# Nyström attention with an MLP behind it: batch 1's first scores and turned block in other places, and batch 2's last spread later

## The chip, the cores and the metric

The kernel runs on one core of a Trainium2 chip. The time is device microseconds of one execution; five executions of the kernel before gave 312.87 to 313.04, with a median of 312.96. The profile is of one such execution. Its engines are TensorE (PE, with its weight loads as PEld), VectorE (DVE), ScalarE (ACT), GpSimd (POOL) and SyncE (SP), which issues most of the transfers.

## The reference

Inputs are q, k and v (8 batches, 8 heads, 576 positions, 64 wide), a layernorm gain g and the weights w_ch1 (512x2048) and w_ch2 (2048x512), all in float32. The output is 8x576x512.

```python
q_lm = q.reshape(B, H, 32, 18, D).mean(axis=3)     # k_lm alike: 32 landmarks
A, Bm, C = sm(q, k_lm), sm(q_lm, k_lm), sm(q_lm, k)  # softmax of scale * a b^T
Z = Bm^T / (norm1(Bm) * norminf(Bm) + 1e-6)
for _ in range(6):
    Z = 2 * Z - Z @ Bm @ Z
x = A @ Z @ C @ v                                   # heads put side by side: 512 wide
xn = (x - mean) / sqrt(var + 1e-6) * g
out = x + relu(xn @ w_ch1) @ w_ch2
```

So each batch has an attention part of many small matrices, with a chain of six dependent steps in its middle, and then 576 rows of a large MLP.

## The kernel before

The order in which each engine gets its instructions is the order in which the program writes them; nothing rearranges them afterwards. Since TensorE works through one list, the art of this kernel is what stands beside what: while one batch's attention waits for VectorE or ScalarE, TensorE is given matmuls of the MLP for rows that are finished already.

**The MLP stream.** The 4608 rows are 36 blocks of 128, in nine groups of four. `mlp()` is a generator. Each of its steps is one matmul: `psh` is the first layer (x is brought to f16 as `xn`, turned as `xnT`, multiplied with `w`, which is w_ch1 scaled by g, and `relu` leaves `hT`), and `pso` the second (from `hT` and w_ch2). `ot` adds x to the result on VectorE, and SP stores it. In the first group the first-layer matmuls take 256 columns, in the later ones 512. The turning of xn is done by TensorE in the first two groups (`psxt`); later a DMA transpose queued on SP does it (L843). From the fifth group on, the second layer is computed in a form with fewer products (`second_layer`, with `pspa`, `pspe` and `pspc`). `fill(n)` takes n steps from the stream.

**The attention.** Batch 0 is computed alone at the start (`attention(0)`, a generator that yields between its stages), batch 1 with the first steps of the stream beside it, and then come the sets (2), (3, 4), (5, 6) and (7) through `attention2`. Two heads of a batch lie side by side on 128 partitions, and four heads make one half, w = 0 or 1.

For batches 0 and 1, `turn_tile(b, w, nm)` turns one half of q or k: nine transposes on TensorE into `pst`, copied by ScalarE into `xT`. For batch 1 it does so in two parts of five and four, with two tiles of the pool `psM`, which has three buffers and serves `psh`, `psxt`, `pso` and the warm matmuls too. `sums(b, w, i, n16)` adds up the landmarks of one half, nine matmuls of 64 columns into `pss`. `scores_of_q(w)` computes eight matmuls into `psa` (in `ps2`, two buffers) and an exponential `ea` on ScalarE. `warm(n, cols)` issues n matmuls on zeros, whose result nobody reads. The iteration step is eight matmuls `psn` on TensorE, then `st` on VectorE, which the next step needs. Behind each of the six steps of batch 0 one more piece is issued, listed in `extra` (L399 and L400), and then what the first sequence of the program (L1117 to L1160) puts there, such as `turn_tile(1, 0, "q")`. Behind the steps come `pszc`, `zcbd` and the rows: `psy` (the product of `zcbd` and `ea`), divided into `xblk`, then `negm`, `xn` and `psxt`.

At the same time SP loads w_ch1 in eight pieces (`wstg`) and GpSimd scales them by g into `w` in pieces of 512 columns; the first `psh` takes them as they come.

**The sets.** For sets 2 and later `Coming` holds the loads, the casts to f16 on GpSimd (`nat`) and the jobs: `xT` by VectorE's own 32x32 transposes, sums `part` by VectorE (`part<-xT`, or `asum` and `s` on GpSimd, turned as `sT`), and the spread: `psl`, two matmuls that put the landmarks in place. `prepare(c, casts, jobs)` takes so many casts and jobs of a set, and issues the next loads on SP as staging buffers come free (tiles `stg` of q, k and v; later sets load into `ring`). `steps` is a table with one row a set and one entry (fills, casts, jobs) for each yield of `attention2`: so many stream steps, then so many casts and jobs of the next set. Ahead of batch 2's attention stand a loop that interleaves its last jobs with six fills each, and the loop at L1208 with two fills of 6 and 15 steps, behind each of which a cast of the set (3, 4) is issued. The last spread of batch 2 comes behind them.

So a number of fills in this table decides both where TensorE's attention matmuls stand among the stream's, and when SP's loads, GpSimd's casts and VectorE's jobs of the next set are issued among the stream's own `xn`, `ot` and stores.

Of the kernel before, what the change touches and what calls it, by code (L numbers as in the profile page):

```python
# [20 lines left out]
def kernel(  # L21
# [52 lines left out]
    def MM(o, l, r, rb=0, cb=0, start=True, stop=True, skip=False):  # L74
        keep(nc.tensor.matmul(o, l, r, start=start, stop=stop, tile_position=(rb, cb),  # L75
                              skip_group_check=(skip or cb != 0)))

    def TR(o, i_, idn):
        keep(nc.tensor.matmul(o, i_, idn, is_transpose=True, tile_position=(0, 0)))  # L79


    def load(src, b, u, queue, t=None):
        t = t or stage.tile([P, 2, NJ, D], FP32, name="stg", tag="stg")
        keep(queue.dma_start(
            out=t[:],
            in_=src[b, 4 * u:4 * u + 4].rearrange("(r e) (t j) d -> (e t) r j d", e=2, j=NJ)))
        return t
# [8 lines left out]
    def load_v(b):  # L96
        for u in range(U):
            raw[b]["v", u] = load(v, b, u, nc.sync)
# [124 lines left out]
    def fetch_w1():  # L223
        coming = []
        for i in range(10):
            if i < 8:
                f, half = divmod(i, 2)
                coming.append(w_stage(w1_src[:, 2 * half:2 * half + 2, ts(f, DM)]))
            if i >= 2:
                f, half = divmod(i - 2, 2)  # L230
                stg = coming.pop(0)
                for c in range(2):
                    k = 2 * half + c
                    pool.tensor_scalar(out=w1_16[:, k, ts(f, DM)], in0=stg[:, c, :],
                                       scalar1=g_sb[:, k:k + 1], scalar2=0.0,
                                       op0=ALU.mult, op1=ALU.add)
# [25 lines left out]
    def warm(n, cols):  # L262
        idle = psM.tile([P, 512], FP32, name="idle", tag="pm")
        for _ in range(n):
            MM(idle[:, 0:cols], zeros[:, 0:P], zeros[:, 0:cols])
# [11 lines left out]
    def sums(b, w, i, n16):  # L277
        for j in range(NJ):
            MM(nat_pss[b, i][:, w, :], n16[:, j, :, :].rearrange("p r d -> p (r d)"),
               pm16[:], start=(j == 0), stop=(j == NJ - 1), skip=True)  # L280

    def turn_part(w, nm, part):
        j0, j1 = ((0, 5), (5, NJ))[part]
        n16 = nat_tiles[1, nm, w]
        if part == 0:
            early_xT[1, nm, w] = aprep.tile([P, NJ, P], FP16, name="xT", tag="xT" + nm,
                                            bufs=5 if nm == "q" else 4)
        pst = psM.tile([P, 5, P], FP16, name="pst", tag="pm")
        for j in range(j0, j1):
            TR(pst[:, j - j0, :], n16[:, j, :, :].rearrange("p r d -> p (r d)"), ident16[:])  # L290
        scalar.copy(early_xT[1, nm, w][:, j0:j1, :], pst[:, 0:j1 - j0, :])

    def turn_tile(b, w, nm):
        i = 0 if nm == "q" else 1
        if b == 1:
            if not i and w == 0:
                pss = ps1.tile([P, 2, U, 64], FP32, name="pss", tag="p1")
                nat_pss[b, 0], nat_pss[b, 1] = pss[:, 0, :, :], pss[:, 1, :, :]
            turn_part(w, nm, 0)
            turn_part(w, nm, 1)  # L300
            return None
        if w == 0:
            nat_pss[b, i] = psM.tile([P, U, 64], FP32, name="pss" + nm, tag="pm")
        n16 = nat_tiles[b, nm, w]
        t = aprep.tile([P, NJ, P], FP16, name="xT", tag="xT" + nm, bufs=5 if nm == "q" else 4)
        early_xT[b, nm, w] = t
        last = (w, i) == (U - 1, 1)
        pst = ps2.tile([P, NJ, P], FP16, name="pst", tag="p2")
        if last:
            sums(b, w, i, n16)  # L310
        for j in range(NJ):
            TR(pst[:, j, :], n16[:, j, :, :].rearrange("p r d -> p (r d)"), ident16[:])
        if not last:
            scalar.copy(t[:], pst[:])
            sums(b, w, i, n16)
        return t, pst

    def attention(b):
# [6 lines left out]
        def p2(shape, dtype, name):  # L325
            return ps2.tile(shape, dtype, name=name, tag="p2")
# [48 lines left out]
        def product(w):  # L375
            if not pscv_:
                pscv_.append(p2([P, W, D + 1], FP32, "pscv"))
            natv = natv_of[b]
            for j in range(NJ):
                for h in range(4):  # L380
                    r, e = divmod(h, 2)
                    rows = ds(64 * e, 64)
                    MM(pscv_[0][ds(32 * h, 32), w, :], ect[w][rows, j, ds(32 * r, 32)],
                       natv[rows, w, j, r, :], rb=64 * e, cb=32 * h,
                       start=(j == 0), stop=(j == NJ - 1), skip=True)

        def scores_of_q(w):
            psa = p2([P, NJ, 64], FP32, "psa")
            for (j0, j1) in ((0, 8), (8, NJ)):
                for h in range(4):  # L390
                    r, e = divmod(h, 2)
                    rows = ds(64 * r, 64)
                    MM(psa[ds(32 * h, 32), j0:j1, :], klm[rows, w, ds(32 * e, 32)],
                       early_xT[b, "q", w][rows, j0:j1, ds(64 * e, 64)], rb=64 * r, cb=32 * h)
            t = aexp.tile([P, NJ * 64], FP16, name="ea", tag="e")
            act(t[:], psa[:].rearrange("p j t -> p (j t)"), AF.Exp, scale=sc_A)
            ea.append(t)

        extra = [None, lambda: product(0), lambda: product(1), lambda: scores_of_q(0),  # L399
                 lambda: scores_of_q(1), None]  # L400
        if first:
            warm(2, 384)
            yield "gram"
# [706 lines left out]
    def fill(n):  # L1110
        for _ in range(n):
            if not next(stream, False):
                return

    def scaled_by_pe():
        psg = psM.tile([P, KCH], FP32, name="psg", tag="pm")
        TR(psg[:], g_rows[:], ident4[:])  # L1117
        dve.tensor_copy(out=g_sb[:], in_=psg[:])

    warm(36, 160)  # L1120
    a0 = attention(0)
    for w, nm in [(w, nm) for w in range(U) for nm in ("q", "k")]:
        last_tile = turn_tile(0, w, nm)
# [6 lines left out]
    for it in range(6):  # L1130
        next(a0)
        if it == 0:
            warm(1, 384)
        elif it == 1:
            scaled_by_pe()
            fetch_w1()
        elif it == 5:
            turn_tile(1, 0, "q")
    next(a0)
    turn_tile(1, 0, "k")  # L1140
    next(a0)
    next(a0)
    sums(1, 0, 0, nat_tiles[1, "q", 0])
    sums(1, 0, 1, nat_tiles[1, "k", 0])
    turn_tile(1, 1, "q")
    sums(1, 1, 0, nat_tiles[1, "q", 1])
    warm(1, 256)
    load_v(1)
    fill(1)
    warm(1, 256)  # L1150
    fill(1)
    turn_tile(1, 1, "k")
    next(a0)
    fill(2)
# [3 lines left out]
    fill(4)  # L1158
    next(a0)
    a1 = attention(1)  # L1160
    next(a1)
    next(a1)
# [9 lines left out]
    def prepare(c, casts, jobs):  # L1172
        for _ in range(casts):
            if c.casts and (c.parts[c.casts[0]][0] == "v" or len(c.n16) < 8):
                c.next_cast()
                while sum(len(x.stg) for x in sets) < (4 if len(sets[1].casts) > 8 else 3):
                    left = [x for x in sets if x.loads]
                    if not left:
                        break
                    left[0].next_load()  # L1180
        for _ in range(jobs):
            c.next_job()
# [23 lines left out]
    while len(sets[0].jobs) > 1:  # L1206
        prepare(sets[0], 1, 1)
        fill(6)  # L1208
    for count in (6, 15):
        fill(count)  # L1210
        prepare(sets[1], 1, 0)

    steps = [[(10, 1, 0), (12, 1, 1)] + 6 * [(6, 1, 1)] + [(8, 1, 1)] + 5 * [(6, 0, 0)]]
    steps += [[(6, 1, 0), (10, 1, 0), (12, 1, 0), (12, 1, 0), (5, 1, 0), (5, 1, 0)] + 4 * [(4, 1, 0)] + [(8, 0, 0), (4, 0, 0), (4, 0, 0), (10, 0, 0)] + 7 * [(8, 1, 1)]]
    steps += [[(12, 1, 0), (14, 1, 1), (16, 1, 1), (16, 1, 1)] + 6 * [(5, 1, 1)] + [(6, 1, 1), (6, 1, 1), (12, 1, 1), (40, 1, 1)] + 7 * [(10, 1, 1)]]
    steps += [[(15, 0, 0), (18, 0, 0)] + 6 * [(8, 0, 0)] + [(10, 0, 0)] + 5 * [(9, 0, 0)]]
    mixing = mixes_of_w2()
# [58 lines left out]
```

## Time and profile before

| what | value |
| --- | --- |
| time of the kernel, median of five | 312.96 us (312.87 to 313.04) |
| time of the profiled execution | 312.96 us |
| its span, first to last instruction | 311.2 us |
| mean granted TensorE clock | 0.998 |
| TensorE busy | 301.7 us, 3475 matmuls |
| VectorE busy | 194.8 us |
| ScalarE busy | 155.7 us |
| GpSimd busy | 141.2 us |
| DMA moved | 50.36 MB, a mean of 162 GB/s |

The page lists busy times by engine, forty slices of the span, the DMA queues, the chain of work that ended last, and groups of instructions. In the lines of a timeline the first two numbers are the start and the time taken, in us; then come engine, line, operation, out<-in, shape and count, and in brackets the idle time ahead of it with what ended it. A run of instructions of one kind without a gap is one line. Times of single matmuls overlap, since they are pipelined: what a matmul costs TensorE in a run is the time from one start to the next, 216 ns for 128x512, 109 for 128x256, 55 for a 128x128 transpose. "issue" is a wait for which the profile shows no releaser.

### The profile page before, as it was taken

To read this page: it belongs to the slowest core of one execution; us is meant where nothing else is said; L and a number is where in the kernel's file an instruction comes from. 1 tells how busy PE (TensorE), PEld (TensorE's weight loads), DVE (VectorE), ACT (ScalarE), POOL (GpSimd) and SP (SyncE) were. 2 spreads that over 40 slices of the span, in tenths; PEclk is the share of its full clock that TensorE was granted. 3 is DMA by queue.
4 is the path that set the end of the run, shared out by engine and by line. 5 is a ranking of instruction groups with operands and counts; after the bars stand their busy time and mean duration, and the time that the engine had idled before them with its cause. 6 is when DMAs were issued, how large, how long until landed. Compare 5 with 4: busy or idle time off the path is not lost.

```text
span 311.2 us, 8486 instructions
## 1 busy us (share of the span) xinstructions
PE 301.7 (97%) x3475; PEld 178.9 (57%) x3475; DVE 194.8 (63%) x525; ACT 155.7 (50%) x309; POOL 141.2 (45%) x191
## 2 busy tenths in 40 slices
PE   7889999999999999999999999999999999999994
PEld 7557764553444534544454468547844874685583
DVE  3667228878785426899257697749635970671364
ACT  2566774469515871177354661693147506405600
POOL 4389878886988493598098412030003240000000
PEclk9999999999999999999999999999999999999999
DMA  7999999999995986750169401530050316105013
GB/s 273 392 386 385 386 388 253 328 343 308 297 194 105 299 239 185 101 205 0 37 96 246 98 1 35 135 68 5 2 135 13 57 43 141 21 3 135 0 36 101
DMA packets 38863, 50.36 MB, mean 162 GB/s; under 512 B 17572, under 2 KB 18088, under 8 KB 38824
## 3 DMA queue, kind: packets, MB, share of 16 engines
q1 hardware_dynamic: 38504, 49.43, 56.5%
q8 instruction: 27, 0.44, 0.6%
q10 hardware_dynamic: 320, 0.39, 0.4%
q14 instruction: 12, 0.10, 0.1%
HBM read 36.70 MB, written 9.44 MB: 148 GB/s over the span
## 4 chain that ended last, share of the span: by engine, by line
PE 92%; DMA 2%; DVE 2%; ACT 1%; issue 0%; SPq 0%
PE psh L75 42%; PE pso L75 18%; PE pspa L75 8%; PE pspe L75 6%; PE pspc L75 6%; PE psy L75 3%; DMA stg<-in_k_dram 2%; PE psn L75 2%; PE pscv L75 2%; PE psec L75 1%; PE psea L75 1%; PE psse L75 1%; DVE xblk L69 1%; PE psxt L79 1%; PE psa L75 0%; PE psl L75 0%
## 5 line engine op out<-in xcount | busy, mean ns | idle before, releaser
L75 PE MATMUL psh<-xnT,w 128*128 128x512 f16 (+1 forms) x640 | 136.7, 358 | 0.5 <-issue 0.2
L69 ACT ACTIVATE hT<-psh 128x512 f16<-128x512 f32 x144 | 84.7, 598 | 71.8 <-PE psh L75 71.2
L75 PEld LDWEIGHTS <-w 128*128 128x128 f16 x640 | 58.9, 98 | 56.2 <-issue 4.9
L75 PEld LDWEIGHTS <-hT 128*128 128x128 f16 x656 | 62.8, 98 | 30.3 <-issue 1.1
L75 PE MATMUL pso<-w,hT 128*128 128x512 f16 x256 | 61.1, 379 | 0.0
L69 POOL TENSOR_SCALAR xn<-xblk,negm,rstd 128x512 f16<-128x512 f32 x20 | 16.9, 855 | 66.9 <-DVE negm L69 33.1
L69 ACT ACTIVATE junk<-xblk,negm 128x512 f16<-128x512 f32 x36 | 25.9, 719 | 18.0 <-POOL negm L69 10.7
L69 DVE SCALAR_TENSOR_TENSOR xblk<-psy,rcpd 128x512 f32<-128x512 f32 (+1 forms) x40 | 27.6, 691 | 1.8
L69 DVE SCALAR_TENSOR_TENSOR st<-st,psn 128x128 f16<-128x128 f16 (+2 forms) x36 | 11.4, 317 | 22.6 <-PE psn L75 22.2
L69 DVE TENSOR_TENSOR hmix<-hT 128x256 f16<-128x256 f16 (+2 forms) x20 | 8.9, 444 | 21.6 <-ACT hT L69 21.6
L69 POOL CAST nat<-stg 128x1152 f16<-128x1152 f32 x15 | 17.1, 1147 | 6.2 <-DMA stg<-in_q_dram 4.1
L69 DVE STREAM_TRANSPOSE xT<-nat 128x576 uint32<-128x576 uint32 x24 | 18.4, 768 | 0.0
L69 DVE TENSOR_REDUCE part<-xT 128x32 f16<-128x576 f16 x26 | 18.3, 745 | 0.1
L69 DVE RECIPROCAL rcpd<-psy 128x8 f32<-128x8 f32 (+1 forms) x40 | 8.1, 202 | 15.6 <-PE psy L75 15.3
L69 DVE SCALAR_TENSOR_TENSOR ot<-pso,rstd,xblk 128x512 f32<-128x512 f32 x16 | 12.0, 747 | 7.8 <-PE pso L75 4.4
L75 PEld LDWEIGHTS <-hmix 128*128 128x128 f16 x160 | 15.6, 98 | 2.0 <-issue 0.2
L69 DVE TENSOR_TENSOR xblk<-pspa,xblk 128x256 f32<-128x256 f32 x38 | 14.0, 417 | 4.2 <-PE pspa L75 4.2
L69 POOL CAST nat<-ring 128x1152 f16<-128x1152 f32 x12 | 13.6, 1145 | 6.7 <-DMA ring<-in_k_dram 4.1
L75 PE MATMUL psy<-zcbd,ea 128*128 128x260 f16 (+1 forms) x80 | 15.4, 277 | 0.0
L69 POOL CAST natv<-stg 128x1152 f16<-128x1152 f32 x10 | 11.5, 1164 | 7.8 <-DMA stg<-in_v_dram 7.4
L75 PEld LDWEIGHTS <-st 32*32 32x32 f16 x448 | 5.6, 90 | 14.5 <-issue 7.6
L69 POOL TENSOR_TENSOR asum<-asum 128x256 f32<-128x256 f32 (+1 forms) x22 | 13.1, 595 | 1.7
(129 smaller groups left out, 383.0 us busy)
## 6 DMA issues: line engine op xcount, KB each, us to landing
wstg<-in_moe_w_ch_dram SPq DMA_DIRECT2D x16, 512.0 KB, 7.0
stg<-in_q_dram SPq DMA_DIRECT2D x10, 576.0 KB, 7.9
stg<-in_k_dram SPq DMA_DIRECT2D x10, 576.0 KB, 7.4
out_dram<-xblk SPq DMA_DIRECT2D x34, 128.0 KB, 2.3
out_dram<-ot SPq DMA_DIRECT2D x32, 128.0 KB, 3.3
stg<-in_v_dram SPq DMA_DIRECT2D x7, 576.0 KB, 9.3
ring<-in_k_dram SPq DMA_DIRECT2D x6, 576.0 KB, 5.1
ring<-in_q_dram SPq DMA_DIRECT2D x6, 576.0 KB, 5.8
```

Of the source, the lines that this page charges most:

```text
L69: return lambda *args, **kw: keep(getattr(self.engine, op)(*args, **kw))
L75: keep(nc.tensor.matmul(o, l, r, start=start, stop=stop, tile_position=(rb, cb), skip_group_check=(skip or cb != 0)))
L79: keep(nc.tensor.matmul(o, i_, idn, is_transpose=True, tile_position=(0, 0)))
```

## The change

Four edits, all of the order of issue; no operation is changed but the size and number of the warm matmuls.

1. `extra` of batch 0: the scores of q's second half go from behind the fifth iteration step to behind the sixth, and in the first sequence the turn of batch 1's first half of q from behind the sixth to behind the fifth.
2. Behind the first two row blocks of batch 0, the turn of q's second half comes first, then three warm matmuls of 512 columns (in all; before there were two of 256, each ahead of a stream step), the load of v and one stream step; the sums of the first halves of q and k stand behind it, then the second stream step, then the sum of q's second half. The sums of k's second half stay.
3. The second fill of the loop at L1208 is 20 steps instead of 15, so a cast of the set (3, 4) and the last spread of batch 2, and all attention behind it, stand five stream steps later.
4. In the second row of `steps` the last seven entries have 7 fills instead of 8, so each of the seven takes one stream step less.

```diff
         extra = [None, lambda: product(0), lambda: product(1), lambda: scores_of_q(0),
-                 lambda: scores_of_q(1), None]
+                 None, lambda: scores_of_q(1)]
...
-        elif it == 5:
+        elif it == 4:
             turn_tile(1, 0, "q")
     next(a0)
     turn_tile(1, 0, "k")
     next(a0)
     next(a0)
+    turn_tile(1, 1, "q")
+    warm(3, 512)
+    load_v(1)
+    fill(1)
     sums(1, 0, 0, nat_tiles[1, "q", 0])
     sums(1, 0, 1, nat_tiles[1, "k", 0])
-    turn_tile(1, 1, "q")
+    fill(1)
     sums(1, 1, 0, nat_tiles[1, "q", 1])
-    warm(1, 256)
-    load_v(1)
-    fill(1)
-    warm(1, 256)
-    fill(1)
     turn_tile(1, 1, "k")
...
-    for count in (6, 15):
+    for count in (6, 20):
         fill(count)
         prepare(sets[1], 1, 0)
...
-    steps += [[(6, 1, 0), (10, 1, 0), (12, 1, 0), (12, 1, 0), (5, 1, 0), (5, 1, 0)] + 4 * [(4, 1, 0)] + [(8, 0, 0), (4, 0, 0), (4, 0, 0), (10, 0, 0)] + 7 * [(8, 1, 1)]]
+    steps += [[(6, 1, 0), (10, 1, 0), (12, 1, 0), (12, 1, 0), (5, 1, 0), (5, 1, 0)] + 4 * [(4, 1, 0)] + [(8, 0, 0), (4, 0, 0), (4, 0, 0), (10, 0, 0)] + 7 * [(7, 1, 1)]]
```

## The prediction

> **What bounds the kernel now.** I read the busy shares and the clock row first, then the chain that ended last, then TensorE's waits, then its timeline wherever it pauses, and the other engines only there.
>
> ```profile
> span 311.2 us, 8486 instructions
> ...
> PE 301.7 (97%) x3475; PEld 178.9 (57%) x3475; DVE 194.8 (63%) x525; ACT 155.7 (50%) x309; POOL 141.2 (45%) x191
> ...
> PEclk9999999999999999999999999999999999999999
> ...
> PE 92%; DMA 2%; DVE 2%; ACT 1%; issue 0%; SPq 0%
> ```
>
> TensorE is busy for 301.7 of 311.2 us and carries 92% of the chain, so it is the bound. It idles 9.5 us: about 1.6 at the start (its first wait) and about 4.2 behind its last matmul, neither touched here, and some 3.7 in small pauses. A change of order can win only from those pauses, or add to them. The change touches the pauses at these places:
>
> ```profile
> 17.79 0.42 PE L75 MATMUL psa<-xT,klm 64*32 64x512 f16 x8 [0.48 <-ACT ea L69]
> ...
> 19.55 0.87 PE L79 MATMUL pst<-ident,nat 128*128 128x128 f16 x9 [0.41 <-ACT xT L69]
> ...
> 21.64 0.41 PE L75 MATMUL pss<-pm,nat 128*128 128x64 f16 x8 [0.48 <-issue]
> ...
> 23.88 0.40 PE L79 MATMUL psxt<-ident,xn 128*128 128x128 f16 x4 [0.40 <-DVE xn L69]
> ...
> 107.58 3.07 PE L75 MATMUL psh<-xnT,w 128*128 128x512 f16 x12
> ...
> 115.06 0.59 PE L75 MATMUL psh<-xnT,w 128*128 128x512 f16 x2 [0.22 <-issue]
> ...
> 160.89 3.41 PE L75 MATMUL pso<-w,hT 128*128 128x512 f16 x15
> 164.41 0.38 PE L75 MATMUL psh<-xnT,w 128*128 128x512 f16 x1
> ```
>
> Two kinds are seen. Some wait for another engine (ea, xT, xn). Others wait for nothing the profile names: at 21.64; inside the twelve psh from 107.58, which at the pace of 0.216 us from start to start would take 2.6 us and took 3.07; and before 115.06. Counted in the trace's list for TensorE, the instructions after these three pauses are numbers 706, 3009 and 3265: multiples of 256 apart, within one. I take them for late instruction blocks, and the DMA queues support it:
>
> ```profile
> q8 instruction: 27, 0.44, 0.6%
> ```
>
> The columns are packets, MB and share. 3475 matmuls and 3475 weight loads over 27 packets make 257 a packet. The packets before the three pauses start at 19.27, 106.95 and 112.51, which is 2.38, 2.46 and 2.55 us before TensorE goes on. So a packet becomes instructions about 2.5 us after its transfer.
>
> **Part 1, scores and first turn swapped (edit 1), sums behind the turned block, longer warm matmuls (edit 2).** The swap puts the nine transposes of batch 1's first block where psa waited 0.48 us for ea, and the second scores where pst waited 0.41 for xT. Rows 1 and 2 (psy, 20.26) move to about 19.6, and the chain psy, xblk, negm, xn, psxt, all behind it, by as much. Against that, the warm work grows from two matmuls of 0.109 (pace of 128x256 in psh rows) to three of 0.216: 0.65 for 0.22, so 0.43 more of work that computes nothing. It stands where TensorE waited for xn (0.40), so most of it replaces waiting. The 27 sums (about 29 ns each) and the transposes (55 each) change place only. Counted through, psxt(0) moves from 22.98 to about 22.2, psxt(1) from 23.88 to 23.25, and psh at 24.83 to about 24.4: the stage wants to gain 0.4 to 0.7.
>
> It cannot keep all of it. The first hidden layer is fed by GpSimd's scaling of w_ch1, and that by the DMA:
>
> ```profile
> 20.84 5.54 POOL L69 TENSOR_SCALAR w<-wstg,g_sb 128x512 f16<-128x512 f32 x8 [0.31 <-DMA wstg<-in_moe_w_ch_dram]
> 26.59 4.96 POOL L69 TENSOR_SCALAR w<-wstg,g_sb 128x512 f16<-128x512 f32 x7 [0.21 <-DMA wstg<-in_moe_w_ch_dram]
> ...
> 29.48 0.82 PE L75 MATMUL psh<-xnT,w 128*128 128x256 f16 x6
> ```
>
> The second run's first four operations feed the hidden columns that TensorE takes from 29.48 on. The last of them ends at 29.54 and its matmul starts at 29.81, with about 0.2 us of slack after the handover. SP issues the loads up to 58 us, those of v by `load_v(1)` among them, in the order of before. So I take −0.2; bounds −0.4 (if a smaller clash of VectorE's xn with GpSimd frees 0.2 more: one w operation takes 0.94 beside an xn, the median is 0.69) and +0.43 (the added warm work all on the path).
>
> The clock row is 9 in all forty slices (mean 0.998) with these pauses in it, so the longer warm work has no clock to win.
>
> **Part 2, the last spread of batch 2 five stream steps later (edit 3).** Five psh steps of 0.216, or 1.08 us, go ahead of psl(0) and everything attention does after it. The work only changes places: 0 by itself. The DMA and GpSimd side shift: on SP, a k load of batches 3 and 4, issued at 62.11, now stands behind two more output stores and the first turning of xn (before 64.50, 1.84 long), so it goes out between 64.5 and 66.3, about 3.4 us later in the middle. GpSimd's cast of that block comes later, with the cast and the xn of a block that stand behind it in order. GpSimd waits 2.08 us for a q load at 72.47 anyway, and xnT of the third group lands at 93.05 for a use at 95.0. With that cover I cost it 0; bounds −0.1 and +0.5.
>
> It also moves the second spread, of batches 3 and 4, by about 1.0:
>
> ```profile
> 95.68 0.49 DVE L69 TENSOR_TENSOR part<-sT 128x64 f16<-128x64 f16 x1
> 96.10 0.74 DVE L69 SCALAR_TENSOR_TENSOR ot<-pso,rstd,xblk 128x512 f32<-128x512 f32 x1
> ...
> 96.23 0.39 PE L75 MATMUL psl<-part,spread 128*128 128x256 f16 x2
> ```
>
> TensorE waits for VectorE here already, about 0.14. VectorE runs nearly without a gap from 87 to 97. Its rows start 1.0 later, and the ot of 0.74 that stood behind the last part now stands ahead of it; the rows' wait of 0.69 and the ot's of 0.26 shrink in return. I get part at about 97.4 for a psl wanted at 97.0: late by 0.4 instead of 0.14, taken as +0.3; bounds −0.14 and +0.7 (the whole ot).
>
> **Part 3, seven fills of 8 become 7 (edit 4).** The shift falls from five steps to −2 (5 − 7) over the rows of batches 3 and 4, and stays near there. Together with edits 1 and 2 it moves where the instruction blocks fall in the stream, and it moves the stores.
>
> The pauses near 109 and 115: one psh in each took 0.522 and 0.613 from start to start instead of 0.216, so 0.31 and 0.40 are lost. The packet for the first came only when a burst of ring loads had drained:
>
> ```profile
> 98.14 1.21 SPq L843 DMA_TRANSPOSE xnT<-xn  x1
> 99.45 1.85 SPq L84 DMA_DIRECT2D ring<-in_k_dram  x2
> 101.40 4.59 SPq L84 DMA_DIRECT2D ring<-in_q_dram  x2
> ```
>
> From 102.5 to 106.6 the DMA moves about 400 GB/s. With the change that block of 256 is entered about 1.2 us later and holds more of the quick attention matmuls, so only about 4.3 us instead of 5.8 lie between asking and needing. The stores ahead of the ring loads leave about 0.75 earlier, the burst drains by about 106.4, the block is there at about 108.9, wanted at 109.0. I take +0.15 where 0.31 stood. For 115.06 the block before it now lasts at least 6.2 us for a need of 5.65, so its 0.40 goes. Sum: −0.56; bounds −0.71 and +0.8 (the packet takes the full 5.8 again: 1.5 late, less the 0.71).
>
> The Trainium skill's page "Runtime: NRT & Kernel Launch", section "Instruction fetch mechanics", says that crossing a block of 256 instructions is "mostly hidden". By it this term would be 0 and the sum −0.17; the rows have three pauses of 0.65, 0.31 and 0.40 at such crossings, so the measurement decides.
>
> Last, 164.41: fifteen pso at pace would end at 164.13; psh of the fifth group waits about 0.27 for the last turning of its xn on the DMA queue. Two steps fewer before it put the second half of the products (pscv, 0.7 us) ahead of that psh, and the wait goes: −0.27; bounds −0.27 and +0.1.
>
> **Sum**, on the profiled execution's 312.96 (span 311.2 and 1.76 around it; it is also the median of the five runs): −0.2 + 0 + 0.3 − 0.56 − 0.27 = −0.73, so 312.2. I give back 0.1 for the two instructions the stream gains and for block crossings elsewhere that I have not followed: **312.3**.
>
> **The rivals.**
> (a) Slower, by the instruction packet at about 109. If the queue delays it for as long as before (5.8 us from asking), TensorE stands 1.5 us there. For it: the DMA is still at about 400 GB/s in that stretch. Against it: the loads come earlier. The sum becomes −0.2 + 0.3 + 0.8 − 0.27 = +0.6, or 313.6; with the early gain lost to the warm work (+0.43) 314.2. It decides from a packet after about 107.2 on.
> (b) No change: the early gain is all eaten (0 for −0.2), the second spread is late by the whole ot (+0.7), the pauses go (−0.56), xnT's wait goes (−0.27): −0.1, or 312.85. For it: VectorE's full stretch. Against it: two of its waits can shrink.
> (c) The late k load carries through GpSimd to xnT of the third group. It has 1.95 between landing and use; a delay of 3.4 that the 2.08 wait does not absorb would cost up to 1.5: about 313.7. Against it: the delayed cast is early in a chain with that wait behind it.
>
> **How the numbers follow.** What a measurement tells from no change is 0.2%, 0.63 us: faster is below 312.33, slower above 313.59. The forecast's case (early gain, pauses mostly gone) has 0.45, of which 0.40 lies below 312.33 and 0.05 above. (b) has 0.25, all within. (a) reaches from 313.6 to 314.2 and has 0.20, of which 0.15 lies above 313.59; (c) has 0.10, all above. That makes 0.40 faster, 0.35 same, 0.25 slower. The range goes from 311.8 (pauses all gone, the second spread no later than now) to 313.9, the middle of (a) and past (c); what is left out is half of (a) and a little below. The likeliest case alone: 311.8 to 312.7.
>
> **What would show it.** Right: psy near 19.6 and psh near 24.4, at 30 only about 0.2 ahead of before; psl of the second spread waiting about 0.4 for part; psh at a pace of 216 ns through 107 to 116; psh of group five directly behind pscv. Wrong: a pause above 0.5 us without a releaser between 98 and 116, waits of GpSimd's xn past 90 us, or new pauses where blocks of 256 now begin.

## The result, and the profile after

The changed kernel takes 313.91 us (median of 53 runs, most between 312.8 and 315.3) and the kernel before 312.88 (94 runs). The ratio is 1.0026, with a 95% interval of 1.0014 to 1.0037: about 0.8 us slower, where 0.6 faster was forecast. (This ratio, and those below, compare executions taken in the same sessions, so they are not the quotients of the medians given.) The profiled execution took 314.74, which is 0.8 above the median; it shows what can happen to this kernel, not its middle.

The page of the changed kernel:

```profile
span 313.0 us, 8490 instructions
...
PE 302.5 (97%) x3476; PEld 178.3 (57%) x3476; DVE 194.4 (62%) x525; ACT 155.8 (50%) x309; POOL 140.5 (45%) x191
...
PE 92%; DMA 2%; DVE 2%; issue 1%; SPq 0%; ACT 0%
```

TensorE is still the bound. "issue" in the chain has come up from 0% to 1%. The list of TensorE's waits from 33 us on names only that:

```profile
engine line waited for: us in total, times, longest us
PE psh L75 <- issue: 1.0, 1, 1.0
PE psea L75 <- issue: 0.7, 1, 0.7
```

TensorE's timeline at the places of the forecast:

```profile
19.50 0.82 PE L75 MATMUL psy<-zcbd,ea 128*128 128x260 f16 x4
...
21.89 0.60 PE L75 MATMUL idle<-zeros 128*128 128x512 f16 x2 [0.66 <-issue]
22.55 0.38 PE L79 MATMUL psxt<-ident,xn 128*128 128x128 f16 x4
...
24.58 0.60 PE L75 MATMUL psh<-xnT,w 128*128 128x256 f16 x4
...
97.41 0.39 PE L75 MATMUL psl<-part,spread 128*128 128x256 f16 x2
...
108.76 0.39 PE L75 MATMUL psh<-xnT,w 128*128 128x512 f16 x1
110.12 2.53 PE L75 MATMUL psh<-xnT,w 128*128 128x512 f16 x11 [0.98 <-issue]
...
165.81 1.46 PE L75 MATMUL psh<-xnT,w 128*128 128x512 f16 x6
...
171.09 0.46 PE L75 MATMUL psea<-xT,lm 32*32 32x288 f16 x14
172.25 0.46 PE L75 MATMUL psea<-xT,lm 32*32 32x288 f16 x18 [0.70 <-issue]
```

Measured over the pace of the matmuls around them, the pauses of the two traces are as follows. (The brackets in the rows show less, since they count from the end of the matmul ahead, and so do the lists of waits.)

| place | before | after |
| --- | --- | --- |
| first iteration step (arrival of the first loads) | 14.46 | 14.71 |
| from there to the 49th psh, at 32 us | 18.03 | 17.69 |
| second spread, 96 or 97 | 0.14 | 0.22 |
| 109 and 115, or 110 | 0.31 + 0.40 | 1.15 |
| first psh of the fourth group, 132 | 0 | 0.25 |
| first psh of the fifth group, 164 | 0.27 | 0 |
| 172 | 0 | 0.98 |
| from the 49th psh to the last | 261.93 | 263.77 |

The early stage gained 0.34. The middle lost 1.84, of which the listed pauses make 1.48; the rest lies in pieces below 0.15 each. So at first sight two late instruction blocks, near 110 and 172, make the loss. The experiments show that this is half of the story.

### The profile page after: what moved, and what is told of

It is laid out like the page before. It is cut to its first block, busy times and chain, and to the rows that moved or that the text cites. A ratio compares the mean times of both kernels' runs of the same rounds, so it can differ in the third digit from the quotient of the medians.

```text
span 313.0 us, 8490 instructions
## 1 busy us (share of the span) xinstructions
PE 302.5 (97%) x3476; PEld 178.3 (57%) x3476; DVE 194.4 (62%) x525; ACT 155.8 (50%) x309; POOL 140.5 (45%) x191
## 4 chain that ended last, share of the span: by engine, by line
PE 92%; DMA 2%; DVE 2%; issue 1%; SPq 0%; ACT 0%
PE psh L75 41%; PE pso L75 18%; PE pspa L75 8%; PE pspe L75 6%; PE pspc L75 6%; PE psy L75 3%; DMA stg<-in_k_dram 2%; PE psn L75 2%; PE pscv L75 2%; PE psec L75 1%; PE psea L75 1%; PE psse L75 1%; PE psxt L79 1%; PE psl L75 1%; DVE xT L69 0%
## 5 line engine op out<-in xcount | busy, mean ns | idle before, releaser
L69 POOL TENSOR_SCALAR xn<-xblk,negm,rstd 128x512 f16<-128x512 f32 x20 | 16.2, 820 | 67.9 <-DVE negm L69 33.1
L69 DVE SCALAR_TENSOR_TENSOR st<-st,psn 128x128 f16<-128x128 f16 (+2 forms) x36 | 11.4, 316 | 22.3 <-PE psn L75 22.2
```

Source lines behind the costliest of these rows:

```text
L69: return lambda *args, **kw: keep(getattr(self.engine, op)(*args, **kw))
```

## The experiments

### Which edits: 1 and 2, or 3 and 4

`early_only` is the change without its two edits of numbers, `late_only` these two alone:

```diff
-    for count in (6, 15):
+    for count in (6, 20):
...
-    steps += [... + 7 * [(8, 1, 1)]]
+    steps += [... + 7 * [(7, 1, 1)]]
```

> Edits 1 and 2 alone. Theory: the early stage gains 0.1 to 0.3 by 32 us and the pauses near 109 and 115 stay as in the kernel before, since the two more instructions move the edges by 2 only: 312.5 to 312.9. Rival (the longer warm work is what costs): 313.3 or more, with psh at 32 us 0.3 or more later than before.

> Edits 3 and 4 alone. Theory: the long pause near 110 is there (0.8 to 1.5 us at one place instead of 0.31 and 0.40 at two) and one near 172 of about 1, so 313.8 to 314.4. Rival (edits 1 and 2 carry the loss): 312.6 to 313.1 with no pause over 0.5 us between 98 and 180.

Edits 1 and 2 alone: 312.87, ratio 0.9974 (0.9947 to 1.0002). The 49th psh starts at 32.06 (before: 32.49); later its trace pauses 0.53 at 109 and 0.85 at 164, and not at 115. Edits 3 and 4 alone: 314.05, ratio 1.0041 (1.0013 to 1.0069). By these ratios the early half gained, though not clear of its interval, and the late half lost more. But the profile of edits 3 and 4 alone has no pause at 110 and only 0.18 at 171. It shows others: 0.42 at 62, where psh waits for VectorE's ot, 0.22 at 96, 0.20 at 132, and 0.59 near 175:

```profile
175.74 0.38 PE L75 MATMUL psl<-part,spread 128*128 128x256 f16 x2 [0.43 <-DVE part L69]
```

### Are the pauses instruction blocks?

Two kernels, the changed one and the one before, got 98 more instructions ahead of everything else, in as many columns of warm work:

```diff
-    warm(36, 160)
+    warm(85, 68)
```

> The changed kernel with the 36 first warm matmuls of 160 columns written as 85 of 68: the same columns in all, 98 more TensorE instructions ahead of everything else, nothing else moved. Theory (late instruction blocks): the changed kernel lost 1.15 us at 110.12 and 0.98 at 172.25 because instruction blocks came late there; with every block edge 98 instructions earlier in the work both pauses go and smaller ones stand elsewhere: 312.0 to 312.9 us. Rival (the moved work waits for other engines or data): nothing but the start changes, the pauses stay at the same matmuls and the time stays at about 313.9.

> The kernel before with the same 98 instructions ahead. Theory: the pauses of 0.65, 0.31 and 0.40 us at 21.64, 109.41 and 115.06 leave these matmuls; 312.0 to 312.9. If the edits themselves are worth nothing apart from the block edges, it and the changed kernel with 98 more agree within 0.4. Rival: pauses and time as in the kernel before, 312.9.

The times went the other way: 314.55 for the changed kernel, ratio 1.0051 (1.0027 to 1.0074), and 316.26 for the one before, 1.0104 (1.0067 to 1.0141). Much of that was lost early. The pause at the early block edge grew to 1.70 in the changed kernel (0.82 without padding) and to 1.33 in the one before (0.65). Behind it the granted clock in both traces is 0.5 for 3.4 us, from 20.9 and from 19.5: nine transposes took 1.05 there in the padded kernel before, and 0.68 at 18.30 without padding. From the first iteration step to the 49th psh it takes 19.59 and 20.03, where it was 17.69 and 18.03. The mean granted clock is 0.995 or less in 10 of the 12 executions of the one, in all six of the other, and in 8 of the 29 of the kernel before taken with them. Why the clock falls there is not shown. The pauses did leave their matmuls, though. In the padded kernel before:

```profile
19.10 0.20 PE L75 MATMUL psa<-xT,klm 64*32 64x64 f16 x1 [1.15 <-issue]
...
19.38 1.05 PE L79 MATMUL pst<-ident,nat 128*128 128x128 f16 x9
...
116.63 0.49 PE L75 MATMUL psea<-xT,lm 32*32 32x288 f16 x27 [1.36 <-issue]
```

The pause of 21.64 moved to a psa at 19.10 and the one of 115.06 to a psea at 116.63, each in the middle of a run of equal matmuls. Counted in TensorE's list they are again instructions 706 and 3265, as in the kernel before without padding. In all the traces, every pause of 0.25 us or more after 30 us that no other engine explains, and that is not at the first psh of a group (which needs its turned xn), stands at 193 modulo 256: 3009 in the changed kernel (psh at 110.12), 4545 (psea at 172.25), 3009 in the padded one before (pscv at 109.89), and so on. Its matmul changes with the padding, its number does not.

The second pair puts 48 quick matmuls of 32x32 on zeros in at about 32 us, behind the early stage:

```diff
     cast_v(1)
     fetch_w2()
+    pad(48)
```

> The changed kernel with 48 matmuls of 32x32 on zeros put in at about 32 us, behind the early stage: 96 more instructions ahead of everything later, about 0.7 us of work at the pace of psn (sixteen in 0.23 us). Theory (late instruction blocks): from the changed kernel's trace, the edges then fall near 104.0, 108.2, 114.5, 121.0, 163.9, 169.4 and 177.1, with 6.4 us or more between asking and needing instead of 5.4 at 110.12; the pauses of 1.15 and 0.98 go: 312.4 to 313.6 in spite of the added 0.7. Rival (waits for data and engines): 0.7 slower than the changed kernel, 314.6, pauses at the same matmuls.

> The kernel before with the same 48 matmuls at about 32 us. Theory: the pauses at 109.41 and 115.06 (0.71 together) go, smaller ones may stand at 107 and 112.6 (5.6 us from asking to needing): 312.8 to 313.6. The difference of the two padded kernels is what the edits do without the blocks: between -0.6 and 0 for the changed one by my forecast, +0.5 or more by the rival. Rival: 313.5 with the pauses where they were.

The changed kernel: 313.89, 1.0042 (1.0025 to 1.0058), with about 0.7 us of added work; the one before: 315.26, 1.0078 (1.0052 to 1.0104). Now the changed kernel is the faster of the two, in this pair by 1.4 us and in the first by 1.7, with intervals of the ratios that just touch in both. The pauses at block edges moved to 3265 (0.28 at a psea) in the one, whose trace also waits 0.61 at 62, 0.58 at 166 and 0.36 at 176, and to 3009 and 3265 (0.35 and 0.27) in the other, which waits 1.62 for a turned xn at 165.62; the forecast had seen that wait as 0.27. But the granted clock differs in this pair: it is 0.995 or less in one of the 12 executions of the changed kernel, and in five of the eight of the other. At a higher clock the medians are 313.88 (eleven) and 314.15 (three), and these are not told apart. So some hundred instructions that compute nothing turn the order of the two medians round, in part by way of the clock. A difference of 0.3% between two orders of this program is not a property of the edits alone.

Then the block at 172 by itself, with 24 more instructions at about 133 us:

```diff
             fill(count)
+            if (c.bs[0], n) == (3, 17):
+                pad(12)
```

> The changed kernel with 12 matmuls of 32x32 on zeros put in at about 133 us, where no block edge is near: 24 more instructions ahead of everything later, about 0.17 us of work. In the changed kernel's trace TensorE asked for the block of the 172.25 pause at 165.02, at the start of 72 quick products; 24 instructions earlier it asks out of the matmuls of 216 ns ahead of these, about 2.5 us sooner, while the pause near 110 keeps its place. Theory (late blocks): no pause over 0.3 us at 170 to 173; 313.0 to 313.6. Rival (that pause is chance, and waits for engines make the loss): 313.9 to 314.2.

```profile
170.34 0.58 PE L75 MATMUL psea<-xT,lm 32*32 32x288 f16 x32
170.85 1.25 PE L75 MATMUL psh<-xnT,w 128*128 128x512 f16 x5
```

The 32 psea run through. The packet came 0.96 us after it was asked for, not 5.00. (The asking is put 95 instructions ahead of a multiple of 256: in the changed kernel's trace the packets of four of the eight blocks needed after 185 us start within 0.2 us of that place.) The time is 313.64, ratio 1.0027 (0.9998 to 1.0056): not told from the changed kernel's. And psl, a few us on, now waits 0.43 for VectorE's part, as it did in `late_only`, and psh waits 0.76 at 62. In the changed kernel part ended 0.06 ahead of psl, which stood later by the late block; so it seems that two stalls stood one behind the other, and that removing the first uncovered the second. The trace has no pause near 110 either, though nothing ahead of that place was moved. And in six other kernels with edits 3 and 4 and no padding the block at 172 came 3.0 to 4.4 us after the asking, for pauses of 0 to 0.38: the 0.98 is the worst of its kind.

### Each number alone

> Edit 3 alone (20 for 15 fills; the rows of batches 3 and 4 and all attention behind batch 2 then stay five stream steps later). If edit 3 carries the loss of edits 3 and 4: 313.7 to 314.3. If it is their sum that matters, because only both together put block edges and loads where they were late: 312.6 to 313.4.

> Edit 4 alone (seven entries of 7 fills for 8; attention of batches 3 and 4 comes up to seven steps earlier in the stream). If edit 4 carries the loss: 313.7 to 314.3, with a long pause at a block edge behind 164 us. If edit 3 does: 312.6 to 313.2.

Edit 3 alone takes 317.92, 1.0161 (1.0118 to 1.0204): over 5 us slower. Edit 4 alone takes 312.92, 0.9998 (0.9967 to 1.0029): no change. The first is neither of the values that I had given. The two executions of edit 3 alone at a granted clock above 0.995 take 315.81 and 316.11, the four others 317.87 to 320.23, so a part of the 5 us goes with the clock. Even its fastest execution, the profiled one, has waits of 0.58 at 132 and 0.97 at 165 for a turned xn, and this one for the spread of batches 5 and 6:

```profile
179.00 0.38 PE L75 MATMUL psl<-part,spread 128*128 128x256 f16 x2 [1.74 <-DVE part L69]
```

Edit 4 takes most of it back. What remains of edit 3 in the whole change is told by leaving it out:

```diff
-    for count in (6, 20):
+    for count in (6, 15):
```

> The change without its third edit (6, 15 for 6, 20). If edit 3 makes the loss: 312.3 to 312.9, as edits 1 and 2 alone and edit 4 alone together would give. If edit 4 does it beside edits 1 and 2: 313.5 or more.

312.34 us, ratio 0.9995 (0.9974 to 1.0017). From 33 us on, the profile has one entry among TensorE's waits:

```profile
engine line waited for: us in total, times, longest us
PE psn L75 <- DVE st L69: 0.4, 1, 0.4
```

So the loss goes with edit 3: with it 1.0026, without it 0.9995, and 1.0041 against 0.9998 where edits 1 and 2 are absent. Neither pair is clear of its intervals; both say about 0.3 to 0.4%, and edit 3 alone leaves no doubt of the sign.

### VectorE beside GpSimd

In six of the eleven kernels with edit 3, psh near 62 waits 0.4 to 1.0 us for ot. (In two of the nine without it psl waits 0.95 at 63, for a sum that stands beside a cast in the same way, so edit 3 does not make this alone.) The timelines of `a_lesswarm`, an experiment told below, show why; GpSimd first, then VectorE:

```profile
58.48 1.15 POOL L69 CAST nat<-stg 128x1152 f16<-128x1152 f32 x1
```

```profile
58.51 1.16 DVE L69 TENSOR_TENSOR part<-sT 128x64 f16<-128x64 f16 x1
...
60.52 0.93 DVE L69 TENSOR_TENSOR part<-sT 128x64 f16<-128x64 f16 x1
61.36 1.40 DVE L69 SCALAR_TENSOR_TENSOR ot<-pso,rstd,xblk 128x512 f32<-128x512 f32 x2
```

The sum part is a small operation: 0.19 or 0.20 in the trace where nothing runs beside it. Here it takes 1.16 and ends at 59.67, 0.04 behind the cast's end at 59.63. It starts 0.03 after the cast; had it started 0.1 before, it would have taken 0.2, as at 58.73 in the changed kernel's own trace:

```profile
58.73 0.20 DVE L69 TENSOR_TENSOR part<-sT 128x64 f16<-128x64 f16 x1
```

```profile
58.82 1.14 POOL L69 CAST nat<-stg 128x1152 f16<-128x1152 f32 x1
```

The Trainium skill, "SBUF — State Buffer", section "SBUF: two separate sides", says that VectorE and GpSimd share a pair of ports as an exclusive lock, that an operation of VectorE with two inputs in SBUF takes part in it against one of GpSimd that reads SBUF, and that "the other fully blocks". These rows agree, to 0.04 us. So do the others: in the twenty traces 143 of these sums start inside a cast of GpSimd, or an operation of it on two inputs, that has 0.2 us or more to go, and every one ends 0.035 to 0.053 us behind its end.

One cast was put on ScalarE, to take the clash away:

```diff
-            if self.bs[0] == 2 and (nm, w) in (('q', 1),):
+            if (self.bs[0], nm, w) in ((2, 'q', 1), (3, 'k', 0)):
                 scalar.copy(t[:], stg[:])
```

> The changed kernel with one cast of a block of k (the first of batches 3 and 4, near 58 us) on ScalarE, which is idle there for 1.4 us at a time, instead of GpSimd. Theory (GpSimd holds VectorE up): the two sums part of sT near 58.6 and 60.4, which take 0.2 us alone and took 0.67 to 1.16 beside a cast in four of the kernels with edit 3, take 0.2 to 0.3, and psh near 62 does not wait for ot (0.42 to 0.96 in those kernels): 313.2 to 313.7. Rival (their length has another cause): they stay long in this profile, 313.9.

```profile
58.55 0.19 DVE L69 TENSOR_TENSOR part<-sT 128x64 f16<-128x64 f16 x1
...
59.59 0.19 DVE L69 TENSOR_TENSOR part<-sT 128x64 f16<-128x64 f16 x1
59.70 0.74 DVE L69 SCALAR_TENSOR_TENSOR ot<-pso,rstd,xblk 128x512 f32<-128x512 f32 x1
```

Both sums are at 0.19 and psh does not wait near 62, so that mechanism is shown. The time is 313.61, 1.0034 (1.0010 to 1.0058): the clash is real, and its removal buys nothing that can be told. A psxt at 60.50 is 0.29 late now, just behind the end of VectorE's ot; 132 has 0.36, and 175 has 0.39.

The mixes of w_ch2 that VectorE makes near 174.5 and 177.7 went to GpSimd, behind its casts of v:

```diff
-    def last_mix_of_w2(k):
-        dve.tensor_tensor(
+    def last_mix_of_w2(k, engine):
+        engine.tensor_tensor(
...
-                            last_mix_of_w2(m - 2)
+                            last_mix_of_w2(m - 2, pool if m > 4 else dve)
```

> The changed kernel with the last two of four mixes of w_ch2 on GpSimd, behind its casts of v, instead of on VectorE near 174.5 and 177.7. Theory: edit 4 lets the loads of v go out earlier, so a cast of v runs beside the mix at 174.5, which takes 1.03 to 1.08 there for 0.41 before; without that mix part is ready about 1 us earlier and psl near 176 never waits for it (0.2 to 0.6 in the kernels with edits 3 and 4 whose block near 172 was in time): 313.2 to 313.8. Rival (blocks alone make the loss): 313.9, psl as in the changed kernel.

313.26, 1.0022 (0.9995 to 1.0048). No psl waits at 175. But in this trace the cast at 58 clashes again (0.81 at 62), and so does the one beside the second spread's part, which takes 1.15 (psl 0.55 late at 98); the block at 110 is 0.88 late.

> Both of these, and the warm matmuls as two of 256 columns. If the clashes of VectorE with GpSimd and the longer warm work make the loss: 312.3 to 313.0. If the blocks near 110 and 172 make it: 313.5 or more.

313.08, 0.9993 (0.9966 to 1.0019): with both clashes and the added warm work out of the way, the kernel is level with the one before, though it keeps edit 3. Its trace still has 0.29 at 132 and 0.39 twice, at 171 (a block) and 175. It does not tell which of the three removals did it; the next experiment, with the short warm work alone, is level too.

### Warm work, the first blocks, and the loads

> The changed kernel with two warm matmuls of 256 columns for the three of 512 (in the place of the three), so 0.43 us less of work and two instructions fewer, as many as in the kernel before. If the longer warm work is hidden behind the block pause near 21.9 and the arrival of w_ch1: psh at 32 us within 0.15 of the changed kernel's, time 313.6 to 314.1. If it is on the path: 0.3 or more earlier, 313.3 to 313.6.

313.22, 1.0003 (0.9978 to 1.0028). From the first iteration step to the first psh it takes 9.79 us, with 9.87 in the changed kernel: the pause at the early block edge grew from 0.82 to 1.26 as the work ahead of it shrank. The 49th psh starts at 32.30 and 32.40, though the first iteration step came 0.80 earlier in this trace: psh waited 0.44 and 0.42 for GpSimd's w. So these traces show the 0.43 us of warm work hidden, the first of the two cases; the time lies below that case's range, and the 0.7 us between the medians is within their intervals.

> Edits 1 and 2 alone, with the first 36 warm matmuls of 160 columns written as 30 of 192: the same columns, 12 instructions fewer ahead of everything. From the trace of edits 1 and 2 alone, the block edge near 109 is then asked for out of the same stretch but needed six matmuls later. Theory: its pause of 0.53 shrinks to 0.3 or less and the early one of 0.84 by up to 0.3: 312.0 to 312.7. Rival: 312.8 as with edits 1 and 2 alone.

312.77, 0.9995 (0.9974 to 1.0015). The pauses at 109 and 115 are gone. A wait of 0.94 for a turned xn at 163.85 stands in their place in this trace, and the median hardly moved.

The experiment `a_fewloads` lets only two loads of later sets be under way at once:

```diff
-                while sum(len(x.stg) for x in sets) < (4 if len(sets[1].casts) > 8 else 3):
+                while sum(len(x.stg) for x in sets) < (4 if len(sets[1].casts) > 8 else 2):
```

> The changed kernel with at most two instead of three loads of later sets under way at once: in the burst of four ring loads near 100 to 106 us the last goes out some 10 us later, and other loads move. Theory: with one load less in its way the block near 110 comes sooner, pause there 0.5 or less instead of 1.15; near 172 it may grow, since a second load of q then stands ahead of it. Time 313.0 to 314.5. Rival (the packet does not depend on the data transfers): 1.0 or more at 110 as before.

318.80, 1.0177 (1.0143 to 1.0210). The block near 110 came 1.14 us after it was asked for and made no pause. But in the seven other kernels with edits 3 and 4 and nothing added ahead of it, it came after 0.99, 1.03, 1.11 and 1.29 in four, without a pause, and after 2.62, 3.02 and 3.25 in three, with one. So this run does not show that the loads are the cause. Its own price is plain: data for batches 5 and 6 come too late, and psl waits 4.56 at 179. Behind that wait the granted clock is 0.5 for 3.4 us, and psh goes at 0.427 from start to start instead of 0.216.

Last, two candidates: the change without edit 3, with the short warm work, and with 12 instructions fewer at the start.

> The change without edit 3 and with two warm matmuls of 256 columns for the three of 512. If the added 0.43 us of warm work is on the path: 311.9 to 312.3, faster than the kernel before by 0.1% or more. If it is hidden behind the block near 21.6 and the arrival of w_ch1: as the change without edit 3, 312.3 to 312.7.

> The same with the first 36 warm matmuls of 160 columns written as 30 of 192, so every block edge is needed six matmuls later. If the pause of about 0.9 us at the early block edge (near 21.6) is on the path, it falls by 0.3 or more: 311.7 to 312.2. If w_ch1 takes the gain back: 312.2 to 312.7.

312.86, 1.0000 (0.9982 to 1.0018), and 312.04, 0.9987 (0.9971 to 1.0004). In both traces the list of TensorE's waits is empty from 33 us on; the spans are 310.3 and 310.0. The second is the best that was run by its median, but not clear of the kernel before. Its early stage does not show why: the pause at the block edge is gone, but psxt waits 1.01 for xn at 21.50, and from the first iteration step to the 49th psh it takes 18.01, with 17.73 in the first.

### The sum over the traces

No single trace stands for a kernel here. So I compare seven traces with edits 3 and 4 (the changed kernel, `late_only`, `a_latepad`, `a_lesswarm`, `a_actcast`, `a_mixpool`, `a_all3`) with seven without edit 3 (the kernel before, `early_only`, `early_30`, `edit4_only`, `no_edit3`, `n_lesswarm`, `n_less30`), and average the pauses of 0.2 us or more at each place. The padded kernels, `edit3_only` and `a_fewloads` are left out.

| place | without edit 3 | with edits 3 and 4 |
| --- | --- | --- |
| 60 to 63: part, ot or xn, VectorE beside GpSimd | 0.17 | 0.50 |
| 95 to 98: second spread, first psh of the third group | 0 | 0.14 |
| 109 to 115: late blocks | 0.18 | 0.50 |
| 132: turned xn of the fourth group | 0 | 0.26 |
| 164 to 177: turned xn, block, part | 0.44 | 0.50 |

(Smaller ones count as 0. Three of the seven have a cast, the mixes or both moved, which makes the column a little low.) The difference is 1.1 us, of the size of edit 3's 1.0 to 1.3. From the 49th psh to the last the seven traces take 261.76 in the mean without edit 3 and 262.97 with it, and the ratios on record have means of 0.9993 (0.9974 to 1.0000, the kernel before as 1) and 1.0021 (0.9993 to 1.0041). So the loss is there whichever way it is counted. It lies in four places and in no single one. Only the one at 132 is in nearly every trace with edit 3 (six of seven, 0.20 to 0.43) and in none without.

That one can be read from SP's list, here of the kernel before and then of the changed one:

```profile
123.88 4.71 SPq L843 DMA_TRANSPOSE xnT<-xn  x3
128.68 1.17 SPq L874 DMA_DIRECT2D out_dram<-ot  x2
```

```profile
125.49 3.46 SPq L843 DMA_TRANSPOSE xnT<-xn  x2
129.05 1.18 SPq L874 DMA_DIRECT2D out_dram<-ot  x2
130.32 1.24 SPq L843 DMA_TRANSPOSE xnT<-xn  x1
```

These are the last three turnings of xn for the fourth group. In all nine kernels without edit 3 no store stands between them; in all eleven with it the last one stands behind two output stores (one in `a_fewloads`). It lands at 132.77 in the changed kernel, for the psh at 132.91; before it landed at 129.87, for a psh at 132.33. Which of edit 3's shifts brings about this order was not tested.

## Why the prediction was wrong

**The bound** was read rightly: TensorE is busy 97% in both, and all that moved are its pauses.

**Part 1** held. psy came at 19.50 (19.6 forecast), psxt at 22.55 and 23.36 (22.2 and 23.25 forecast), psh at 24.58 (24.4), with the first loads 0.25 later in that execution. Over ten traces with edits 1 and 2 at a clock of 0.995 or more, without padding ahead of that place, the 49th psh starts at 32.25 in the mean, over three without at 32.49: 0.24 gained, where −0.2 was taken. The arrival of w_ch1 is a cap: in six of the ten, psh pauses by 0.15 to 0.44 near 27 or 29 us.

**Part 2 is the step that failed**: "The work only changes places: 0 by itself", with bounds of −0.1 and +0.5. It was costed by the cover of one chain (the k load, GpSimd's wait, xnT of the third group). That cover held in the changed kernel, but barely: from landing to use it is 0.61, where it was 1.95, and in `late_only` the psh at 95.84 is 0.22 late, 0.24 behind such a landing and with no releaser in the profile. The five steps moved every later operation of VectorE and GpSimd against the stream, in a stretch where VectorE has no slack and one of its operations takes 0.2 or 1.2 us by whether it starts just ahead of a cast or just behind. In place of 0 the runs showed about 1 us beside the other edits (1.1 by the pauses, 1.0 and 1.3 by the two pairs of ratios), and 5 for edit 3 alone. The term +0.3 for the second spread was too large for this trace (0.08) and too small for one other (0.55). That part beside GpSimd is slow stood in the row that I quoted (0.49; the one at 93.79, not quoted, took 1.04), and I read it as the operation's own time.

**Part 3** had the mechanism right and the size wrong. The window of the block near 110 was forecast at 4.3 us and was 4.2 (asked at 104.75, wanted 1.15 before 110.12). (The 5.8 that the prediction sets beside it is the time from asking to arrival; from asking to needing it was 5.5 before.) The packet was taken to come at 106.4 and came at 107.76, 3.02 us after asking: 1.15 for the 0.15 taken, inside the bounds, and rival (a)'s mechanism with its condition (a packet after 107.2) met. But in four of the seven traces with edits 3 and 4 the packet came 1.0 to 1.3 after asking, so this size changes from run to run. The pause at 115 went, as forecast. The reserve of 0.1 for "block crossings elsewhere that I have not followed" was the other wrong size: 0.98 at 172 in this trace, from a packet 5.00 us after asking, in a stretch (165 to 172.5) in which the queue of the data is 96.6% busy.

**164**: the wait went in the changed kernel, −0.27 as forecast; 132, one group earlier, came up for 0.25.

Rival (c) was near in kind, a turned xn that comes late by a changed order, but mostly one group later, by SP's list, and at 0.26 in place of 1.5.

## What to carry to other kernels

When a program's order is fixed per engine, a shift of a few steps is not free because "the work only changes places": list for the stretches behind it which engine has no slack, and which of its operations have two prices. Where pauses have no releaser, count the instructions: if they share a remainder, the edits also move block edges, and a 0.3% difference can turn its sign with a hundred instructions of padding, so compare at two paddings, and at like granted clocks, before one believes it. And average over several traces where one kernel's runs scatter by 1%.

## What was not expected of the hardware

TensorE's late instruction blocks: a packet of 256 instructions becomes usable 2.2 to 2.7 us after its transfer starts, in every pause of 0.25 us or more at these places. In the changed kernel it starts 0 to 1.9 us after the asking where the DMA is quieter (blocks after 185 us), and up to 5.9 where loads run; in a padded kernel it was 7.1. "Runtime: NRT & Kernel Launch" of the Trainium skill, under "Instruction fetch mechanics", calls the crossing "mostly hidden"; here single ones cost up to 1.7 us. In the pauses of 0.25 us or more, 4.2 to 8.9 us lay between asking and needing (288 instructions).

Ninety-eight instructions ahead of a kernel, in the same number of columns, made it 1.0% slower (1.0104); 2.0 us of the 4.6 in the profiled execution are lost in the early stage, where the granted clock is 0.5 for 3.4 us.
